# Output products of a Strassen scheme in fp32, with the weights standing or moving, and a transpose before the store

## The chip, the cores and the metric

The kernel runs on one core of a Trainium2 chip. The time is the device time of one execution in microseconds (us), and the kernel before takes 1200.21 us, the median of 3 runs (1199.89 to 1200.61).

The core's engines each take their own instructions in order and wait for one another by semaphores. TensorE (PE) multiplies: it loads an operand of 128x128 that stands (PEld, the weight load), and another one, up to 512 columns here, moves through it. Results go to PSUM banks of 128x512 values. VectorE (DVE) and ScalarE (ACT) take them on from there, GpSimd (POOL) and SyncE (SP) mostly issue DMAs.

## The reference

Batches of tokens go through an attention with a small state, then through two feed-forward parts (B = 8, 512 tokens and 32 state rows a batch, 512 features, inner sizes 2048 and 1024):

```python
x = attention(x, state)                    # (8 * 544, 512)
h = np.maximum(x @ w_in, 0.0)
x = h * h @ w_out                          # 4352 x 512
a = x @ w1
b = x @ w2
out = (a * b @ w3) @ w_out2                # 4352 x 512, float32
```

## The kernel before

Everything is float32. A product is made from HI and LO parts: HI is the value cast to the short form fp32r (a cast on ScalarE, L83), LO is the remainder (a subtraction on VectorE, L84). Three passes, HI·HI, LO·HI and HI·LO, make up a product (`PASSES`). Both halves of that are written into one tile; this is called a split.

The kernel has four stages: attention, the first feed-forward part (L586), the merging of w3 and w_out2 into one matrix w34 (L1123), and the last part, which takes the final 380 us or so. Only that last part is touched.

In it, batches go in pairs (c0, c1), four of them: (3,4), (5,6), (7,2), (0,1). The inner dimension of 1024 is taken in two halves, s = 0 and s = 1; the second goes through the pairs backwards, so that its pairs 1 to 4 are (0,1), (7,2), (5,6), (3,4). Each pair does two things:

- Four **quads** (`quad`, m = 0 to 3), which make a·b for 128 of the 512 inner features of the half and the tokens of a pair. A quad is a Strassen scheme of seven products, each six matmuls with 512 columns (L1301), into the banks A (qa), D (qd), E (qe) and C (qc). ScalarE copies a sum out (L1309, tiles s0 to s3), VectorE adds another bank to it (L1313), multiplies two of them into q1 and q0 (L1333, L1341), and forms differences of them (L1255).
- **out_pair**, the product of a·b with w34, again Strassen with seven products over pairs of batches and halves of the 256 output columns (NH): A11·B11, S1·T1, S4·B22, A12·B21, S2·T2, S3·T3, A22·T4, in that order, into banks oa, od, oe and oc. Each has 24 matmuls with 256 columns (L1461): the tokens' operand z stands and the weights move. Its operands z (B11, T1, B22, B21, and later T2, T3, T4) exist for idx 0, from the quads m = 0 and 1, and for idx 1, from m = 2 and 3. Their splits are made by `to_z` and `late_z` in six tiles c1 to c6, each holding one operand at a time.

Results of 128 tokens x 256 columns, two to a tile of 128x512, are collected in PSUM, copied out (L1484), added to (L1491) and stored. In the first half the pair that comes first goes to a scratch and is added in by the last pair of the second half, which loads it (`fetch`). All other pairs go to the output in the first half (L1499, on SP) and in the second are accumulated into it by DMA (L1501, on POOL). For batches 0 and 1 (c < BLK) the tokens stand in another order in the tile than for the others.

During an out_pair, the loads and splits for the next pair's quads (`make_pair`, tiles yq) run as `jobs`. Some weights change place within an out_pair: `load_turn` overwrites part 1 of w34 (L1426) after S4·B22, for S3·T3.

The order of instructions on each engine is set by a scheduler while the kernel is built, within the waits that code gives (`tc.issue_after`) and those that tiles give when they are reused.

Of the kernel before, what the change touches and what calls it, by code (L numbers as in the profile page):

```python
# [8 lines left out]
F32 = mybir.dt.float32  # L9
# [4 lines left out]
ALU = mybir.AluOpType  # L14
# [6 lines left out]
def kernel(  # L21
# [17 lines left out]
    nc = tc.nc  # L39
    B, H, S, D = x.shape  # L40
# [5 lines left out]
    P = 128  # L46
# [1250 lines left out]
    def quad(c0, c1, m, behind=None):  # L1297
        def product(ps, w, v, first=True, last=True):
            for kt in range(2):
                for k, (wi, vi) in enumerate(PASSES):  # L1300
                    nc.tensor.matmul(  # L1301
                        ps, W[w, kt][:, wi, m * P:(m + 1) * P], Y[v, kt][:, vi, :],
                        start=(first and kt == 0 and k == 0), stop=(last and kt == 1 and k == 2),
                        skip_group_check=True,
                    )

        def kept(i, ps):
            t = bp.tile([P, 512], F32, tag=f"s{i}", bufs=1 + (i == 0), name=f"s{i}")
            left["copy"] = nc.scalar.copy(t, ps)  # L1309
            return t  # L1310

        def plus(t, ps):
            nc.vector.tensor_tensor(out=t, in0=ps, in1=t, op=ALU.add)  # L1313

        A, D, E, C = bank_m("qa"), bank_y(m % 2, "qd"), bank_y(2, "qe"), bank_y(3, "qc")
        product(A, "A11", "B11", last=False)
        p1 = kept(0, A)
        with tc.issue_after(behind.ins) if behind else nullcontext():
            product(D, "S1", "T1", last=False)
        p5 = kept(1, D)  # L1320
        with tc.issue_after(behind.ins) if behind else nullcontext():
            product(E, "A12", "B21")
        plus(p1, E)
        product(A, "S2", "T2", first=False, last=False)
        u2 = kept(2, A)
        product(D, "S4", "B22", first=False)
        plus(u2, D)
        product(C, "A22", "T4")
        product(A, "S3", "T3", first=False)
        u3 = kept(3, A)  # L1330
        plus(p5, A)
        q1 = bp.tile([P, 512], F32, tag="qd" if m % 2 else "qb", bufs=1 if m % 2 else 2, name="q1")
        nc.vector.tensor_tensor(out=q1, in0=u2, in1=p5, op=ALU.mult)  # L1333
        if parts and m in (0, 2):
            add_behind(q1[:, :1])
        plus(u3, C)
        if m % 2:
            q0 = bp.tile([P, 512], F32, tag="qc", bufs=2, name="q0")
        else:
            q0 = pa.tile([P, 512], F32, tag="r", bufs=2, name="q0")  # L1340
        nc.vector.tensor_tensor(out=q0, in0=p1, in1=u3, op=ALU.mult)  # L1341
        return to_z(m, q0, q1)
# [84 lines left out]

    OUTS = {"11": (0, 0), "12": (1, 0), "21": (0, 1), "22": (1, 1)}
    AT = {"11": ("s0", "s1"), "22": ("yo", "yo"), "12": ("r", "r"), "21": ("qc", "qc")}
    TWO = ("s0", "yo", "r", "qb", "qc")  # L1430

    def place(tag, name):
# [2 lines left out]

    def out_pair(c0, c1, s, jobs, last, first, more):
        ends = s == 1 and not more
        jobs, gate = list(jobs), left["copy"]

        def do(n):  # L1440
# [12 lines left out]
            return w34_t[u][:, {"A11": 0, "A12": 2, "A22": 3}.get(w, 1)]  # L1453

        def product(ps, w, v, first=True, last=True):
            for tp in range(2):
                for t in (2 * tp, 2 * tp + 1):
                    for idx in range(NB):
                        rhs = moving(w, s * NB + idx, idx)
                        for k, (vi, wi) in enumerate(PASSES):  # L1460
                            nc.tensor.matmul(  # L1461
                                ps[tp][:, t % 2 * NH:(t % 2 + 1) * NH], Z[v, idx][:, vi, t * P:(t + 1) * P], rhs[:, wi],
                                start=(first and t % 2 == 0 and idx == 0 and k == 0), stop=(last and idx == NB - 1 and k == 2),
                                skip_group_check=True,
                            )
# [10 lines left out]
        def keep(block, ps, tp0=0):  # L1476
            ts = []
            for tp, p in enumerate(ps, tp0):
                if ends:
                    t = o_in.pop((block, tp))  # L1480
                    nc.vector.tensor_tensor(out=t, in0=p, in1=t, op=ALU.add)
                else:
                    t = place(AT[block][tp], "o")
                    nc.scalar.copy(t, p)  # L1484
                ts.append(t)
            return ts

        def put(block, ts, ps, tp0=0):
            c, i = where(block)
            for tp, t in enumerate(ts, tp0):  # L1490
                nc.vector.tensor_tensor(out=t, in0=ps[tp - tp0], in1=t, op=ALU.add)  # L1491
                if s == 0 and first:
                    nc.sync.dma_start(scr(c, i, tp), t)
                    continue
                rows_t = "(p j) e -> p j e" if c < BLK else "(j p) e -> p j e"
                dst = out[c * T:c * T + S, i * NH:(i + 1) * NH].rearrange(rows_t, j=J)[:, 2 * tp:2 * tp + 2]
                src = t.rearrange("p (j e) -> p j e", j=2)
                if s == 0 or ends:
                    nc.sync.dma_start(dst, src)  # L1499
                else:  # L1500
                    nc.gpsimd.dma_start(dst, src, accum_op=ALU.add)  # L1501

        for block in ("11", "22"):
            fetch(block)
# [155 lines left out]
```

## Time and profile before

| | |
|---|---|
| median of 3 runs | 1200.21 us (1199.89 to 1200.61) |
| the profiled execution | 1200.36 us, of which the span is 1198.5 us |
| granted TensorE clock over the span | 0.999 |
| TensorE busy | 1187.9 us |
| VectorE busy | 934.0 us |
| ScalarE busy | 694.4 us |

The page of the profile first gives the busy time of each engine, then the chain of waits that ended last, as a share of the span. Timelines show when each group of instructions begins, how long it lasts from its first start to its last end, and what the idle time before it waited for. PE's matmuls overlap, so that the distance from start to start is what counts there. Weight loads have rows of their own, PEld.

### The profile page before, as it was taken

What the parts mean: (1) busy time and instruction counts of PE and PEld (TensorE: products, weight loads), DVE (VectorE), ACT (ScalarE), POOL (GpSimd) and SP (SyncE); (2) the same over time, 40 slices, a digit from 0 to 9 for tenths busy, and PEclk for the clock granted to TensorE, in tenths of its full rate; (3) what the DMA queues carried; (4) which work ended last, traced back from release to release, by engine and by line L of the source; (5) the groups of instructions that cost most, each with busy time, mean ns of one, the idle gap of its engine ahead of it and who ended that gap; (6) DMA issues with size and microseconds to landing.
All of it is one profiled execution on the core that took longest, in us unless ns stands there. A gap on an engine that the chain in (4) does not pass through costs nothing.

```text
span 1198.5 us, 18846 instructions
## 1 busy us (share of the span) xinstructions
PE 1187.9 (99%) x6988; PEld 981.0 (82%) x6988; DVE 934.0 (78%) x1671; ACT 694.4 (58%) x1263; POOL 160.9 (13%) x225
## 2 busy tenths in 40 slices
PE   7999999999999999999999999999999999999998
PEld 5677777777777777777888888989898989898988
DVE  7989878778878673677778986969696958787877
ACT  6877556555556565777767653636454525354542
POOL 0000013324331100013221001010000001211210
PEclk9999999999999999999999999999999999999999
DMA  8675768946795923356697686574141631625334
GB/s 252 137 231 195 186 216 226 198 126 179 162 219 155 265 100 110 107 120 110 97 210 231 239 217 119 138 125 133 47 152 34 214 112 38 139 45 131 58 66 142
DMA packets 172533, 179.25 MB, mean 150 GB/s; under 512 B 90760, under 2 KB 124296, under 8 KB 171912
## 3 DMA queue, kind: packets, MB, share of 16 engines
q1 hardware_dynamic: 132936, 112.75, 32.0%
q0 software_dynamic: 37488, 61.88, 24.8%
q10 hardware_dynamic: 2016, 3.41, 0.8%
q8 instruction: 55, 0.90, 0.3%
q14 instruction: 38, 0.31, 0.1%
HBM read 114.43 MB, written 74.06 MB: 157 GB/s over the span
## 4 chain that ended last, share of the span: by engine, by line
PE 97%; ACT 1%; DVE 1%; DMA 0%; issue 0%; SPq 0%; DVEq 0%
PE y L586 22%; PE qa L1301 11%; PE qd L1301 7%; PE oa L1461 6%; PE od L1461 4%; PE ps_w L1123 4%; PE qc L1301 4%; PE qe L1301 4%; PE qa L957 3%; PE ps_sw L499 3%; PE oe L1461 2%; PE ab L1367 2%; PE qd L957 2%; PE oc L1461 2%; PE y L558 1%; PE po L1400 1%
## 5 line engine op out<-in xcount | busy, mean ns | idle before, releaser
L586 PE MATMUL y<-ghl,wo 128*128 128x512 f32 x1152 | 280.1, 392 | 0.1
L586 PEld LDWEIGHTS y<-ghl,wo 128*128 128x128 f32 x1152 | 214.3, 188 | 58.0 <-issue 12.6
L1309 ACT COPY s<-qa 128x512 f32<-128x512 f32 x96 | 56.4, 588 | 179.4 <-PE qa L1301 179.4
L1301 PE MATMUL qa<-yq,wq 128*128 128x512 f32 x576 | 143.9, 389 | 0.0
L530 DVE TENSOR_TENSOR ghl<-r,ghl 128x512 fp32r<-128x512 f32 (+1 forms) x112 | 72.6, 648 | 72.9 <-ACT ghl L529 63.7
L1301 PEld LDWEIGHTS qa<-yq,wq 128*128 128x128 f32 x576 | 107.6, 188 | 21.9
L1301 PE MATMUL qd<-yq,wq 128*128 128x512 f32 x384 | 97.4, 389 | 0.0
L84 DVE TENSOR_TENSOR z<-q,z 128x512 fp32r<-128x512 f32 x112 | 74.2, 686 | 24.3 <-ACT z L83 24.3
L1301 PEld LDWEIGHTS qd<-yq,wq 128*128 128x128 f32 x384 | 72.1, 188 | 15.0
L83 ACT CAST z<-q 128x512 fp32r<-128x512 f32 x112 | 68.2, 626 | 19.7 <-PE oe L1461 7.4
L1313 DVE TENSOR_TENSOR s<-qa,s 128x512 f32<-128x512 f32 x32 | 22.1, 692 | 69.8 <-ACT s L1309 69.8
L1501 POOL DMA_DIRECT2D out_dram<-o x24 | 28.8, 1617 | 310.3 <-DVE o L1491 310.3
L528 ACT ACTIVATE r<-r 128x512 f32<-128x512 f32 (+1 forms) x112 | 67.5, 603 | 4.2 <-DVE yo L597 1.5
L529 ACT CAST ghl<-r 128x512 fp32r<-128x512 f32 (+1 forms) x112 | 66.1, 591 | 2.8
L84 DVE TENSOR_TENSOR yq<-yraw,yq 128x512 fp32r<-128x512 f32 x98 | 64.2, 684 | 1.1 <-ACT yq L83 1.1
L83 ACT CAST yq<-yraw 128x512 fp32r<-128x512 f32 x98 | 59.2, 625 | 7.9 <-DVE yraw L1230 5.5
L1301 PE MATMUL qe<-yq,wq 128*128 128x512 f32 x192 | 48.7, 389 | 0.0
L1301 PE MATMUL qc<-yq,wq 128*128 128x512 f32 x192 | 48.7, 389 | 0.0
L1123 PE MATMUL ps_w<-wo,w3T 128*128 128x512 f32 x192 | 44.1, 390 | 0.0
L1255 DVE TENSOR_TENSOR q<-q,q 128x512 f32<-128x512 f32 x64 | 43.1, 684 | 0.0
L1301 PEld LDWEIGHTS qe<-yq,wq 128*128 128x128 f32 x192 | 36.0, 188 | 7.5
L1301 PEld LDWEIGHTS qc<-yq,wq 128*128 128x128 f32 x192 | 36.0, 188 | 7.5
(708 smaller groups left out, 2503.4 us busy)
## 6 DMA issues: line engine op xcount, KB each, us to landing
yraw<-yscr SPq DMA_DIRECT2D x56, 256.0 KB, 5.6
raw<-in_moe_w_out_dram SPq DMA_DIRECT2D x16, 512.0 KB, 4.6
yscr<-yo SPq DMA_DIRECT2D x32, 256.0 KB, 3.3
raw<-in_moe_w_dram POOLq DMA_DIRECT2D x64, 128.0 KB, 4.0
raw<-in_moe_w_dram POOLq DMA_DIRECT2D x16, 512.0 KB, 7.7
raw<-in_moe_w_in_dram SPq DMA_DIRECT2D x12, 512.0 KB, 4.4
xb<-in_x_dram SPq DMA_DIRECT2D x96, 64.0 KB, 3.1
X<-in_x_dram SPq DMA_DIRECT2D x12, 512.0 KB, 9.0
```

What stands on the lines that cost most here:

```text
L83: nc.scalar.copy(hi, src)
L84: return nc.vector.tensor_tensor(out=lo, in0=src, in1=f32(hi), op=ALU.subtract)
L528: nc.scalar.activation(r[:, :n], r[:, :n], ACTF.Square)
L529: casts.append(nc.scalar.copy(t[:, HI, :n], r[:, :n]))
L530: done.append(nc.vector.tensor_tensor(out=t[:, LO, :n], in0=r[:, :n], in1=f32(t[:, HI, :n]), op=ALU.subtract))
L586: mm = nc.tensor.matmul(y_ps[c, d][:, :n], wo_t[f][:, wi, d * P:(d + 1) * P], t[:, gi, :n], start=(f == f0 and k == 0), stop=(f == f1 - 1 ...
L957: nc.tensor.matmul(ps[d], wt[:, wi, d * P:(d + 1) * P], v[:, kt, gi, :], start=(first and kt == 0 and k == 0), stop=(last and kt == 1 and ...
L1123: mm = nc.tensor.matmul(ps, t[:, wi, (j % 4) * P:(j % 4 + 1) * P], wo2_t[j][:, vi, :], start=(j == 0 and k == 0), stop=(j == N1 - 1 and k ...
L1255: return nc.vector.tensor_tensor(out=t, in0=a, in1=b, op=ALU.subtract)
L1301: nc.tensor.matmul(ps, W[w, kt][:, wi, m * P:(m + 1) * P], Y[v, kt][:, vi, :], start=(first and kt == 0 and k == 0), stop=(last and kt == ...
L1309: left["copy"] = nc.scalar.copy(t, ps)
L1461: nc.tensor.matmul(ps[tp][:, t % 2 * NH:(t % 2 + 1) * NH], Z[v, idx][:, vi, t * P:(t + 1) * P], rhs[:, wi], start=(first and t % 2 == 0 an ...
```

## The change

For three of the four pairs of each half (in the code `turn`: all but the first of the first half, and the last of the second, which go on as before) the product's operands change roles. The weights stand: 128 of 256 columns of w34, every second one, in two groups d = 0, 1. The tokens' z moves, 512 columns at once. So a product has 12 matmuls with 512 columns instead of 24 with 256, and results lie with the columns on partitions and the tokens along the tile.

The first half's turned results go to the scratch, and the second half accumulates the scratch into its own tile (POOL, L1523). A tile is then turned, in the quads m = 0 (blocks 11 and 12) and m = 1 (22 and 21) of the pair that follows: `turn_out` transposes it in 32x32 blocks on VectorE (L1440) into a tile "turned", whose tags are c6, c5, c4 and c2, and stores it in four DMAs on SP (L1443), each with runs of 64 values (256 bytes). In all 24 transposes of 128x512 and 48 such stores.

```diff
@@ -1329,6 +1329,8 @@
         product(A, "S3", "T3", first=False)
         u3 = kept(3, A)
         plus(p5, A)
+        for block in to_turn[:2]:
+            turn_out()
         q1 = bp.tile([P, 512], F32, tag="qd" if m % 2 else "qb", bufs=1 if m % 2 else 2, name="q1")
         nc.vector.tensor_tensor(out=q1, in0=u2, in1=p5, op=ALU.mult)
         if parts and m in (0, 2):
@@ -1427,6 +1429,18 @@
 
     OUTS = {"11": (0, 0), "12": (1, 0), "21": (0, 1), "22": (1, 1)}
     AT = {"11": ("s0", "s1"), "22": ("yo", "yo"), "12": ("r", "r"), "21": ("qc", "qc")}
+    TURNED = {"11": 6, "12": 5, "22": 4, "21": 2}
+    to_turn = []
+
+    def turn_out():
+        block, c, i, ts = to_turn.pop(0)
+        o = bp.tile([P, 4 * J, NS, 2], F32, tag=f"c{TURNED[block]}", bufs=1, name="turned")
+        for d, t in enumerate(ts):
+            src = t.rearrange("p (j k n) -> p k n j", j=J, n=NS // J) if c < BLK else t
+            nc.vector.transpose(out=o[:, :, :, d], in_=src)
+        dst = out[c * T:c * T + S, i * NH:(i + 1) * NH].rearrange("(k p) (a e) -> a p k e", p=NS, a=4)
+        for a in range(4):
+            nc.sync.dma_start(dst[a], o[a * NS:(a + 1) * NS].rearrange("p k e d -> p k (e d)"))
     TWO = ("s0", "yo", "r", "qb", "qc")
 
     def place(tag, name):
@@ -1435,6 +1449,7 @@
 
     def out_pair(c0, c1, s, jobs, last, first, more):
         ends = s == 1 and not more
+        turn = not ends and not (s == 0 and first)
         jobs, gate = list(jobs), left["copy"]
 
         def do(n):
@@ -1453,6 +1468,17 @@
             return w34_t[u][:, {"A11": 0, "A12": 2, "A22": 3}.get(w, 1)]
 
         def product(ps, w, v, first=True, last=True):
+            if turn:
+                for d in range(2):
+                    for idx in range(NB):
+                        lhs = moving(w, s * NB + idx, idx).rearrange("p i (n d) -> p i d n", d=2)
+                        for k, (vi, wi) in enumerate(PASSES):
+                            nc.tensor.matmul(
+                                ps[d], lhs[:, wi, d], Z[v, idx][:, vi, :],
+                                start=(first and idx == 0 and k == 0), stop=(last and idx == NB - 1 and k == 2),
+                                skip_group_check=True,
+                            )
+                return
             for tp in range(2):
                 for t in (2 * tp, 2 * tp + 1):
                     for idx in range(NB):
@@ -1480,7 +1506,8 @@
                     t = o_in.pop((block, tp))
                     nc.vector.tensor_tensor(out=t, in0=p, in1=t, op=ALU.add)
                 else:
-                    t = place(AT[block][tp], "o")
+                    tag = "tp" if turn and s == 1 and AT[block][tp] == "s1" else AT[block][tp]
+                    t = place(tag, "o")
                     nc.scalar.copy(t, p)
                 ts.append(t)
             return ts
@@ -1489,16 +1516,18 @@
             c, i = where(block)
             for tp, t in enumerate(ts, tp0):
                 nc.vector.tensor_tensor(out=t, in0=ps[tp - tp0], in1=t, op=ALU.add)
-                if s == 0 and first:
+                if s == 0 and (first or turn):
                     nc.sync.dma_start(scr(c, i, tp), t)
+                    continue
+                if turn:
+                    nc.gpsimd.dma_start(t, scr(c, i, tp), accum_op=ALU.add)
                     continue
                 rows_t = "(p j) e -> p j e" if c < BLK else "(j p) e -> p j e"
                 dst = out[c * T:c * T + S, i * NH:(i + 1) * NH].rearrange(rows_t, j=J)[:, 2 * tp:2 * tp + 2]
                 src = t.rearrange("p (j e) -> p j e", j=2)
-                if s == 0 or ends:
-                    nc.sync.dma_start(dst, src)
-                else:
-                    nc.gpsimd.dma_start(dst, src, accum_op=ALU.add)
+                nc.sync.dma_start(dst, src)
+            if turn and s == 1:
+                to_turn.append((block, c, i, ts))
 
         for block in ("11", "22"):
             fetch(block)
```

The order of the engines changes in these places. On ScalarE, at the start of the output products of the second pair of the second half, in before (q is a quad's product, z its split; z_10742 and z_10746 are B11 and T1 for idx 1):

```order
L1309 COPY s0_10759<-qa_10749 128x512
L1309 COPY s1_10767<-qd_10750 128x512
L83 CAST z_10742<-q0_10740 128x512
L1309 COPY s2_10782<-qa_10749 128x512
L83 CAST z_10746<-q0_10740 128x512
L1309 COPY s3_10803<-qa_10749 128x512
L83 CAST yq_10880<-yraw_10599 128x512
L83 CAST yq_10883<-yraw_10600 128x512
L1484 COPY o_10839<-oa_10813 128x512
L83 CAST yq_10932<-yraw_10599 128x512
```

and in after (z_10387 is B22 for idx 0, z_10636 is T4 for idx 0, z_10458 is B11 for idx 1):

```order
L1309 COPY s3_10519<-qa_10465 128x512
L83 CAST yq_10572<-yraw_10301 128x512
L83 CAST yq_10575<-yraw_10302 128x512
L83 CAST yq_10612<-yraw_10301 128x512
L83 CAST z_10387<-q1_10382 128x512
L83 CAST yq_10615<-yraw_10302 128x512
L83 CAST z_10586<-q0_10292 128x512
L83 CAST yq_10670<-yraw_10301 128x512
L83 CAST z_10547<-q1_10522 128x512
L83 CAST z_10636<-q0_10385 128x512
L83 CAST yq_10673<-yraw_10302 128x512
L83 CAST z_10458<-q0_10456 128x512
```

The casts for B11 and T1 for idx 1, which stood between the copies of the last quad, now stand eleven and twelve rows behind its last copy s3 (T1's is the row after the last one shown).

On TensorE, at the same place, in before (oa and od are the banks of A11·B11 and S1·T1; z_10592 is B11 for idx 0, z_10742 for idx 1):

```order
L1301 MATMUL qa_10749<-yq_10524,wq_9774 128x512 x3
L1301 MATMUL qa_10749<-yq_10527,wq_9777 128x512 x3
L1461 MATMUL oa_10813<-w34b_9780,z_10592 128x256 x3
L1461 MATMUL oa_10813<-w34b_9782,z_10742 128x256 x3
...
L1461 MATMUL oa_10814<-w34b_9780,z_10592 128x256 x3
L1461 MATMUL oa_10814<-w34b_9782,z_10742 128x256 x3
```

and in after:

```order
L1476 MATMUL oa_10529<-z_10294,w34b_9552 128x512 x3
L1476 MATMUL oa_10530<-z_10294,w34b_9552 128x512 x3
L1476 MATMUL od_10554<-z_10298,s12_9724 128x512 x3
L1476 MATMUL od_10555<-z_10298,s12_9724 128x512 x3
L1476 MATMUL oe_10618<-z_10392,w34b_9552 128x512 x3
L1476 MATMUL oe_10619<-z_10392,w34b_9552 128x512 x3
L1476 MATMUL oc_10698<-z_10636,w34b_9552 128x512
L1476 MATMUL oc_10699<-z_10636,w34b_9552 128x512
L1476 MATMUL oa_10529<-z_10458,w34b_9554 128x512 x3
L1476 MATMUL oa_10530<-z_10458,w34b_9554 128x512 x3
L1476 MATMUL od_10554<-z_10462,s12_9727 128x512 x3
L1476 MATMUL od_10555<-z_10462,s12_9727 128x512 x3
```

idx 0 and idx 1 no longer alternate. What needs idx 0 of B11 (z_10294), T1 (z_10298) and B21 (z_10392) stands ahead, two matmuls of A22·T4 follow, and then idx 1 of A11·B11 and S1·T1 (z_10458, z_10462).

On VectorE, in the first quad of the same pair, in before:

```order
L1313 TENSOR_TENSOR s2_10563<-qd_10531,s2_10563 128x512
L1313 TENSOR_TENSOR s1_10548<-qa_10530,s1_10548 128x512
L1313 TENSOR_TENSOR s3_10584<-qc_10533,s3_10584 128x512
L1333 TENSOR_TENSOR q1_10587<-s2_10563,s1_10548 128x512
L1341 TENSOR_TENSOR q0_10590<-s0_10540,s3_10584 128x512
L84 TENSOR_TENSOR z_10592<-q0_10590,z_10592 128x512
```

and in after (o_10029 and o_10031 are the tiles of block 11, o_10148 and o_10150 those of 12):

```order
L1313 TENSOR_TENSOR s2_10251<-qd_10219,s2_10251 128x512
L1440 STREAM_TRANSPOSE turned_10275<-o_10029 128x512
L1313 TENSOR_TENSOR s1_10236<-qa_10218,s1_10236 128x512
L1440 STREAM_TRANSPOSE turned_10275<-o_10031 128x512
L1440 STREAM_TRANSPOSE turned_10282<-o_10148 128x512
L1440 STREAM_TRANSPOSE turned_10282<-o_10150 128x512
L1335 TENSOR_TENSOR q1_10289<-s2_10251,s1_10236 128x512
L1313 TENSOR_TENSOR s3_10272<-qc_10221,s3_10272 128x512
L1313 TENSOR_TENSOR s0_10321<-qe_10313,s0_10321 128x512
L1343 TENSOR_TENSOR q0_10292<-s0_10228,s3_10272 128x512
```

Four transposes now stand between the quad's additions and its products q1 and q0.

## Rows read from the trace of the kernel before

**Rows 1.** The page: span, busy time and share of each engine, chain
```profile
span 1198.5 us, 18846 instructions
...
PE 1187.9 (99%) x6988; PEld 981.0 (82%) x6988; DVE 934.0 (78%) x1671; ACT 694.4 (58%) x1263; POOL 160.9 (13%) x225
...
PE 97%; ACT 1%; DVE 1%; DMA 0%; issue 0%; SPq 0%; DVEq 0%
```

**Rows 2.** Windows: length, busy us of PE, PEld, DVE, ACT, POOL, clock, DMA share, GB/s
```profile
1057.25:1077.40 20.15, 20.15 (x169) 20.15 (x168) 19.34 (x33) 14.51 (x27) 3.85 (x4) 1.00 0.31 55
1019.10:1057.25 38.15, 38.15 (x171) 31.59 (x169) 27.19 (x45) 14.38 (x25) 5.75 (x5) 1.00 0.48 107
```

**Rows 3.** Timeline of PE: start, length, engine, line, operation
```profile
1055.89 1.52 PE L1301 MATMUL qa<-yq,wq 128*128 128x512 f32 x6
1057.25 3.04 PE L1461 MATMUL oa<-w34b,z 128*128 128x256 f32 x24
1060.12 3.04 PE L1461 MATMUL od<-s,z 128*128 128x256 f32 x24
```

**Rows 4.** Timeline of ACT, last quads and first output products
```profile
1051.13 0.62 ACT L83 CAST z<-q 128x512 fp32r<-128x512 f32 x1
...
1053.85 0.62 ACT L83 CAST z<-q 128x512 fp32r<-128x512 f32 x1
...
1057.45 0.59 ACT L1309 COPY s<-qa 128x512 f32<-128x512 f32 x1 [2.98 <-PE qa L1301]
1057.93 1.14 ACT L83 CAST yq<-yraw 128x512 fp32r<-128x512 f32 x2
1058.97 0.59 ACT L1484 COPY o<-oa 128x512 f32<-128x512 f32 x1
```

**Rows 5.** Timeline of DVE, first output products
```profile
1058.07 0.69 DVE L1313 TENSOR_TENSOR s<-qa,s 128x512 f32<-128x512 f32 x1 [2.27 <-ACT s L1309]
1058.67 0.68 DVE L1313 TENSOR_TENSOR s<-qc,s 128x512 f32<-128x512 f32 x1
1059.27 0.68 DVE L1333 TENSOR_TENSOR q<-s,s 128x512 f32<-128x512 f32 x1
```

**Rows 6.** Weight loads in one pair, by line: busy us, mean ns | idle
```profile
L1301 PEld LDWEIGHTS qd<-yq,wq 128*128 128x128 f32 x48 | 9.0, 188 | 1.9
...
L1461 PEld LDWEIGHTS od<-s,z 128*128 128x128 f32 x24 | 3.0, 192 | 0.0
```

**Rows 7.** Line 296, transposes in the attention stage: ns min/median/max
```profile
L296 DVE STREAM_TRANSPOSE xT<-xb x24: 666/700/712, 63.7 to 410.6; 128x512 f32<-128x512 f32 x24
```

**Rows 8.** Timelines of POOL, DVE, ACT and PE in a pair's first quads
```profile
1020.65 4.82 POOL L1501 DMA_DIRECT2D out_dram<-o  x4 [0.62 <-DVE o L1491]
...
1030.71 0.68 DVE L1333 TENSOR_TENSOR q<-s,s 128x512 f32<-128x512 f32 x1
...
1031.61 0.59 ACT L1309 COPY s<-qd 128x512 f32<-128x512 f32 x1 [0.77 <-PE qd L1301]
...
1034.13 1.52 PE L1301 MATMUL qd<-yq,wq 128*128 128x512 f32 x6
```

**Rows 9.** Line 1501, the accumulating DMAs
```profile
DMA to landing us min/median/max: 4.3/6.6/9.5
```

**Rows 10.** Line 301, loads of X of 512 KB
```profile
DMA to landing us min/median/max: 4.8/9.0/15.0
```

**Rows 11.** DMA from 8 to 20 us, loads of X and a weight
```profile
DMA packets 6225, 3.19 MB, mean 266 GB/s; under 512 B 5446, under 2 KB 5446, under 8 KB 6224
```

**Rows 12.** DMA from 1042 to 1057 us
```profile
DMA packets 0, 0.00 MB, mean 0 GB/s; under 512 B 0, under 2 KB 0, under 8 KB 0
```

**Rows 13.** Line 1426, reloads of the weights that turn
```profile
DMA to landing us min/median/max: 3.1/3.9/7.6
```

**Rows 14.** Timeline of all engines, start of the last pair's output products
```profile
1173.77 3.04 PE L1461 MATMUL oa<-w34b,z 128*128 128x256 f32 x24
...
1174.59 0.69 DVE L1313 TENSOR_TENSOR s<-qa,s 128x512 f32<-128x512 f32 x1 [2.27 <-ACT s L1309]
```

## The prediction

> **What bounds the kernel now.** First the page's busy shares and its chain of waits: TensorE is busy 99% of a span of 1198.5 us and carries 97% of the chain, and no other engine has more than 78% [rows 1]. So a saving on TensorE counts in full, and so does each wait that it is given. Then the windows of one pair: 20.15 us of output products, all of it TensorE, with VectorE busy 19.34 of them; and four quads in 38.15 us, with VectorE at 27.19 [rows 2]. VectorE thus has 11 us of room in the quads and under one in the output products. Last the timelines around the start of such a phase, where the order of ScalarE and VectorE decides when TensorE gets its next operand [rows 3 to 5]. I follow the second pair of the second half, whose output products begin at 1057.25.
>
> **Fewer and longer matmuls.** A product of 24 matmuls with 256 columns goes from 1057.25 to 1060.12, 2.87 us or 120 ns each; six with 512 columns go from 1055.89 to 1057.25, 227 ns each [rows 3]. Twelve of those take 2.72 us. I take 0.16 us a product (the whole phase gives the same: 20.15 against 84 x 0.227 = 19.04 us), and six turned pairs of seven products make 42: **-6.7 us**.
> The Trainium skill ("TensorE: Matmul & The Clock Gate", Back-to-back issue gap) gives an isolated warm spacing of N/2.4 + 2.5 ns, 109 and 216 ns here; an estimate from it is 2.62 against 2.59 us a product, 1.2 us in all, and the sum below would be +10.0. It adds that a stream with weight loads goes otherwise; the rows, with 120 and 227, decide for this kernel.
>
> **Weights with a stride.** The standing operand is now every second column, 8 bytes apart; no load of before is like it. Today's loads take 188 to 192 ns and already follow at 120 ns in the output products [rows 3, 6]. Lower bound: nothing. Upper bound: twice the time, a pitch of 240 instead of 227 ns, 13 ns x 504 = +6.6 us. A gain is excluded, since a load of the same 128 columns isn't the limit at 227. I take nothing, because a load at 120 ns has 107 ns to spare under a 512-column matmul.
>
> **Transposes.** 24 of them, four blocks for each of three pairs, two tiles a block. The kernel has the same operation on the same shape, in its attention stage, at 0.70 us [rows 7]: 16.8 us of VectorE, 5.6 in each of three groups of quads, which go from 27.2 to 32.8 busy of 38.15. The order puts them in quads 0 and 1. In quad 0 the product q1, at 1030.71 in before [rows 8], comes three transposes later, near 1032.5 at its end; ScalarE's next copy into s1 (1031.61 before) must wait for it and ends near 1033.2, and TensorE adds to that bank at 1034.13 [rows 8]. About 0.9 us of slack is left, so 0; if the cover were gone, the cost would be some tenths in each of the three pairs.
>
> **Stores and accumulation.** The first half stores its three turned pairs to scratch instead of the output, same bytes on the same queue: 0. In the second half POOL's accumulation now goes into the tile. It takes 4.3 to 9.5 us to land today [rows 9]; a pair's last four are issued from 1020.65 to 1025.5 [rows 8], at most 9.5 us later they are in, and quad 1, which turns their blocks, ends near 1038 (38.15 / 4 a quad): 0. The 48 new stores of 128 KB have 256-byte runs, and the tile each leaves (c6, c5, c4, c2) is overwritten by a split of the same pair. Near them are the loads of X, also 256-byte runs: 512 KB land in 9.0 us at the median [rows 10], and a window full of such packets, 5446 of 6225, moved 3.19 MB in 12 us [rows 11]. A pair's 2.1 MB would need 8 us at that rate; they are issued from about 1031 on, and the DMA queues are empty from 1042 to 1057 [rows 12]. I take them as done by 1054, before the splits that follow: 0. Nothing below 0 is to be had from any of this, since none of it stands on TensorE's path now.
>
> **Splits that move.** This is the term that decides. Because the turned tiles lie in c2, c4 and c5, the scheduler puts the splits of B11 and T1 for idx 1, and of B22 for idx 0, behind the last quad wherever the quads carry transposes: pairs 2, 3 and 4 of the second half. In before ScalarE casts two of them at 1051.13 and 1053.85, long ahead of the first output product [rows 4]. In after they stand behind the copy s3 and a run of ten casts. The engines take their work in order, so that is the price:
> - ScalarE begins s3 at 1057.45, the next cast at 1057.93, and two casts take 1.04 us up to 1058.97, so 0.52 each [rows 4].
> - TensorE fills with 18 matmuls on operands that are there: 18 x 0.227 = 4.08, to 1061.33. Then come two that need the ninth cast (T4), which starts at 1057.93 + 8 x 0.52 = 1062.09 and ends 0.62 later: **1.4 us of waiting**. They last till 1063.16.
> - B11 needs the eleventh cast, started at 1063.13 and done at 1063.75: **0.6**. Its LO part is VectorE's, done 0.69 later, after one matmul of 0.23: **0.5**. Five more matmuls last till 1065.6.
> - T1's LO part stands four VectorE operations behind B11's. At their pitch of 0.60 (1058.07, 1058.67, 1059.27) [rows 5] it starts at 63.75 + 2.4 = 1066.15 and ends at 1066.85; TensorE has one HI matmul to do and is there at 1065.8: **1.1**.
> - The weights that turn are reloaded after S4·B22 and needed by S3·T3, 18 matmuls or 4.1 us later instead of 5.7; the reload lands in 3.1 to 7.6, median 3.9 [rows 13]: 0 to 3.5, I take **0.3**, near the median.
> Sum 3.9 us. The next pair has the same list, but one cast ahead (T2, into the tile that holds T1 of idx 0) waits for TensorE to have read that, near 1060: +0.5, **4.4**. In the last pair the columns stay 256: its 18 matmuls of fill last only 2.2 us, to 1173.77 + 2.16 = 1175.9, and two more to 1176.2; B11's LO half is the sixth on VectorE from 1174.59 [rows 14], so 1174.59 + 3.0 + 0.69 = 1178.3: 2.1, and 0.8 more where B21's LO comes late: **2.9**. Together **+11.2 us**. From half of it (fill that I count too short, casts in another order) to one and a half: 5.6 to 16.8.
> In the first half and in pair 1 of the second nothing is postponed, and the order there is as before: 0.
>
> **Sum.** -6.7 + 11.2 = +4.5. The profiled execution took 1200.36 us (span 1198.5 and 1.86 around it) and the median is 1200.21, 0.15 less; from the profile 1204.9, from the median **1204.7 us**. Some 0.2%, 2.4 us, is what a measurement of this kernel can tell from no change.
>
> **The rivals.**
> - *No stall (faster).* The splits are covered: ScalarE gets through its ten casts before the fill ends. Only the -6.7 stands: **1193.5 us**. For it: ScalarE is busy 14.51 of 20.15 us in this phase [rows 2], so it has the time, and a trace may show that casts ahead of z were ready long before and ran in the gaps of the last quad. Against it: the order is fixed, s3 waits for the last quad's bank until 1057.45, and eleven casts would have to take 0.35 us each to be in time where the rows show 0.52. It decides below 0.35. Chance 0.11.
> - *Half of the stall.* The waits overlap with one another or with the next quads: 5 to 9 us of stall, 1198.5 to 1202.6. It is the same mechanism at a smaller price, chance 0.14.
> - *Strided weights at twice the time.* +6.6 on top: **1211.3 us**. For it: nothing in the trace is like it. Against: loads hide at 120 ns now. It decides once a load sets a pitch above 227 ns. Chance 0.08.
> - *Short-run stores late.* If the 512 KB blocks go one after another at X's 9.0 us [rows 10], the fourth is stored at 1031 + 4 x 9 = 1067, and the cast into c2 starts then and not at 1063.1: +3.7, the same in the next pair, +6.4 in the last, whose fill is shorter: **1218.5 us**. For it: X's landings reach 15.0 us [rows 10]. Against: several were in flight there at once, and the queues are empty for 15 us here. Chance 0.05. The Trainium skill ("DMA: Bandwidth & Descriptors", Specifications) asks for at least 512 bytes for line rate and has a read-modify-write below it, which would make writes slower than these reads; no row here shows a store in such runs.
>
> **How the numbers follow.** Forecast 0.62 (1202.6 to 1210), half 0.14, no stall 0.11, strided 0.08, stores 0.05. Faster by over 0.2%: no stall and the lower end of half, 0.13. Within it: the rest of half and the forecast's lowest edge, 0.15. Slower: 0.72. The range 1198 to 1212 leaves out no stall, late stores and the far ends, under 0.2.
>
> **What would show it.** In the trace of after: twelve matmuls a product at 227 ns in the first half, phases near 19.0 us; loads near 190 ns. In the second half, from pair 2 on, TensorE idle some 4 us in the first half of the output products, released by ScalarE's and VectorE's split (z). Transposes at 0.70 us inside the quads with no wait of TensorE on them. The forecast is wrong if those phases show no idle TensorE (then 1193.5), if the casts into c2 and c4 wait for a DMA (then 1218), or if the pitch is over 235 ns (then 1211).

## The result, and the profile after

The changed kernel takes 1211.18 us, the median of 5 runs (1210.14 to 1212.79), against 1200.61 (1199.89 to 1200.77) of the kernel before: 1.009 times, 95% interval 1.0075 to 1.0105. It is slower by 10.6 us where the prediction had 4.5. The profiled execution took 1211.18 us too, its span is 1209.3.

The page of the changed kernel, its busy shares and its chain of waits:

```profile
PE 1190.0 (98%) x6484; PEld 957.7 (79%) x6484; DVE 952.9 (79%) x1695; ACT 695.5 (58%) x1263; POOL 152.9 (13%) x225
...
PE 93%; DVE 3%; ACT 2%; DMA 1%; issue 1%; SPq 0%; ACTq 0%; DVEq 0%
```

Beside [rows 1], TensorE's share of the chain has fallen from 97% to 93%, and VectorE and ScalarE have moved in. Windows of four phases of output products, pairs 1, 2, 3 and 4 of the second half (columns as in [rows 2]):

```profile
997.53:1017.13 19.60, 19.60 (x86) 16.20 (x84) 18.39 (x31) 14.51 (x27) 2.62 (x3) 1.00 0.24 50
1056.63:1080.28 23.65, 21.18 (x87) 16.08 (x85) 20.39 (x33) 16.44 (x30) 1.93 (x3) 1.00 0.16 39
1118.30:1142.76 24.46, 21.19 (x87) 16.08 (x85) 20.39 (x33) 16.54 (x30) 1.94 (x3) 1.00 0.16 41
1180.80:1205.10 24.30, 22.14 (x169) 21.70 (x167) 21.66 (x36) 6.90 (x12) 0.00 (x0) 0.93 0.49 158
```

Pair 1, where nothing is postponed, takes 19.60 us with TensorE busy throughout; before, such a phase took 20.15 [rows 2]. Pairs 2 and 3 take 23.65 and 24.46, one quad matmul of 0.23 among each, so 3.8 and 4.6 over pair 1. Pair 4, whose products are as before, takes 24.3 where the kernel before needs 20.4, from 1173.77 [rows 14] to the end of its last matmuls (timeline of PE, before):

```profile
1192.23 1.96 PE L1554 MATMUL oc<-w34b,z 128*128 128x256 f32 x15
```

The timeline of PE in pair 2 shows where the 3.8 us lie (start, length, operation, and in brackets the idle time ahead and what ended it):

```profile
1056.63 1.56 PE L1476 MATMUL oa<-z,w34b 128*128 128x512 f32 x6
1058.03 1.56 PE L1476 MATMUL od<-z,s 128*128 128x512 f32 x6
1059.43 1.56 PE L1476 MATMUL oe<-z,w34b 128*128 128x512 f32 x6
1062.17 0.74 PE L1476 MATMUL oc<-z,w34b 128*128 128x512 f32 x2 [1.18 <-ACT z L83]
1063.21 0.51 PE L1476 MATMUL oa<-z,w34b 128*128 128x512 f32 x1 [0.30 <-ACT z L83]
1063.94 1.43 PE L1476 MATMUL oa<-z,w34b 128*128 128x512 f32 x5 [0.22 <-DVE z L84]
1065.31 0.50 PE L1476 MATMUL od<-z,s 128*128 128x512 f32 x1
1066.59 1.43 PE L1476 MATMUL od<-z,s 128*128 128x512 f32 x5 [0.78 <-DVE z L84]
```

It is the list of the prediction: 18 matmuls on idx 0, a wait for T4's cast, one for B11's cast, one for its LO half, one for T1's. Read by starts the waits are longer than the bracketed idle: 18 matmuls at 0.233 end their share at 1060.83, and the next starts at 1062.17, 1.34 us later. The others, read in the same way, are 0.57, 0.50 and 1.05, with 0.2 more ahead of T1's first matmul.

One wait was not in the sum. TensorE is in quad 1 of pair 2, and VectorE still has two transposed blocks ahead of quad 0's q1 (timelines of DVE, ACT and PE):

```profile
1028.99 3.09 DVE L1440 STREAM_TRANSPOSE turned<-o 128x512 f32<-128x512 f32 x3
1032.00 0.65 DVE L1335 TENSOR_TENSOR q<-s,s 128x512 f32<-128x512 f32 x1
...
1032.74 0.58 ACT L1309 COPY s<-qd 128x512 f32<-128x512 f32 x1 [3.89 <-DVE q L1335]
...
1033.38 1.65 PE L1301 MATMUL qd<-yq,wq 128*128 128x512 f32 x6 [1.12 <-ACT s L1309]
```

These transposes take 1.10 us each, against 0.70 in [rows 7]; in a row they follow one another at about 1.0 us (ns, minimum, median and maximum of the eight in these quads):

```profile
L1440 DVE STREAM_TRANSPOSE turned<-o x8: 1065/1102/1123, 1027.1 to 1040.4; 128x512 f32<-128x512 f32 x8
```

The quads of pair 2 last 39.5 us (1017.13 to 1056.63) instead of 38.1.

Put together, measured against predicted:

| term | predicted | measured |
|---|---|---|
| six turned phases, without waits | -6.7 | 6 x (19.60 - 20.15) = -3.3 |
| quads of pair 2 | 0 | +1.4 |
| waits in the output products of pair 2 | +3.9 | +3.8 |
| of pair 3 | +4.4 | +4.6 |
| of pair 4 | +2.9 | +3.9 |
| sum | +4.5 | +10.4 |

The spans differ by 10.8 us; the last 0.4 lie in small shifts elsewhere.

### The profile page after: what moved, and what is told of

It reads as the page before. It is cut to its first block, busy times and chain, and to the rows that moved or that the text cites. A ratio compares the mean times of both kernels' runs of the same rounds, so it can differ in the third digit from the quotient of the medians.

```text
span 1209.3 us, 17962 instructions
## 1 busy us (share of the span) xinstructions
PE 1190.0 (98%) x6484; PEld 957.7 (79%) x6484; DVE 952.9 (79%) x1695; ACT 695.5 (58%) x1263; POOL 152.9 (13%) x225
## 4 chain that ended last, share of the span: by engine, by line
PE 93%; DVE 3%; ACT 2%; DMA 1%; issue 1%; SPq 0%; ACTq 0%; DVEq 0%
PE y L586 20%; PE qa L1301 11%; PE qd L1301 7%; PE oa L1476 4%; PE ps_w L1123 4%; PE qc L1301 4%; PE qe L1301 3%; PE qa L957 3%; PE od L1476 3%; PE ps_sw L499 3%; PE ab L1369 2%; PE qd L957 2%; PE oa L1487 1%; PE oc L1476 1%; PE y L558 1%; PE oe L1476 1%
## 5 line engine op out<-in xcount | busy, mean ns | idle before, releaser
L1301 PEld LDWEIGHTS qd<-yq,wq 128*128 128x128 f32 x384 | 71.8, 188 | 16.8 <-ACT s L1309 1.9
L1523 POOL DMA_DIRECT2D o<-oscr x24 | 20.8, 1056 | 325.9 <-DVE o L1518 322.8
```

The lines of the kernel that those rows point to most:

```text
L1301: nc.tensor.matmul(ps, W[w, kt][:, wi, m * P:(m + 1) * P], Y[v, kt][:, vi, :], start=(first and kt == 0 and k == 0), stop=(last and kt == ...
```

## The experiments

The theory: the order of the engines costs the waits, because the turned tiles lie in c2, c4 and c5 and the scheduler thinks that their stores hold these long; the stores, the transposes and the weights themselves don't. Rivals: the stores really hold the tiles, or the transposes or the strided weights cause the waits. Two smaller questions are why a matmul takes 233 instead of 227 ns and why some transposes take 1.10 us.

**Without the stores.**

```diff
         for a in range(4):
-            nc.sync.dma_start(dst[a], o[a * NS:(a + 1) * NS].rearrange("p k e d -> p k (e d)"))
+            pass
```

> The changed kernel without its 48 new stores of turned tiles (those rows of the output are not written); the transposes stay. With the stores gone the scheduler leaves the splits of B11, T1 and B22 in their old place between the copies of the last quad. Theory (order): the waits of 3.8, 4.6 and 3.9 us in the output products of pairs 2, 3 and 4 of the second half vanish, 12.3 us, and the time goes from 1211.2 to about 1199; the 1.3 us in quad 1 of pair 2 stays. Rival (the transposes or the strided weights cause the waits): within 2 us of the changed kernel.

Measured: 1199.27 us, 0.9987 of the kernel before (0.9978 to 0.9997). The splits stand between the copies again, and pairs 2 and 3 take the 19.6 us of pair 1, without a wait (windows of those two phases):

```profile
1056.29:1075.88 19.59, 19.59 (x86) 16.20 (x85) 18.40 (x31) 14.51 (x27) 2.58 (x3) 1.00 0.25 51
1114.18:1133.78 19.60, 19.60 (x86) 16.21 (x85) 18.40 (x31) 14.51 (x27) 2.58 (x3) 1.00 0.24 51
```

So the 24 transposes and the strided weights, both still there, don't make the waits in the output products; the wait of 1.12 us in quad 1 of pair 2 stayed. Whether the stores make them by traffic or by the order is left to the next one.

**The order held, the stores in place.** The scheduler is told (`issue_after`) to queue some instructions behind others of their engine. The last line holds each output matmul behind the one before it.

```diff
-            left["copy"] = nc.scalar.copy(t, ps)
+            with behind_split({(3, 2): ("B11", 1), (3, 3): ("T1", 1)}.get((m, i))):
+                left["copy"] = nc.scalar.copy(t, ps)
...
-        nc.vector.tensor_tensor(out=q1, in0=u2, in1=p5, op=ALU.mult)
+        with behind_split({3: ("T1", 1, LO)}.get(m)):
+            nc.vector.tensor_tensor(out=q1, in0=u2, in1=p5, op=ALU.mult)
...
+                            with behind_mm():
```

> The changed kernel with all its stores where they are; only the order is held: casts of B11 and T1 for idx 1 ahead of the copies s2 and s3 of the last quad, their LO halves ahead of q1 on VectorE, and the output matmuls in the order written. Theory (the order alone costs it; the tiles are free, since the stores land in about 3 us): as without the stores, 1211.2 - 12.3, about 1199. Rival (the stores hold c2, c4 and c5): the casts then wait for a DMA in the last quad and the time stays over 1206.

Measured: 1201.09 us, 1.0002 of before (0.9993 to 1.0012), 10 us less than the changed kernel with every store in place. In pair 2 the cast of T1 waits for its operand on VectorE, not for a DMA, and in the changed kernel itself the DMA queues are all but empty after the stores (timeline of ACT here, then two rows of the changed kernel: its DMA line from 1046 to 1057, and the landing of the 48 stores):

```profile
1056.07 0.62 ACT L83 CAST z<-q 128x512 fp32r<-128x512 f32 x1 [2.17 <-DVE q L1269]
```

```profile
DMA packets 19, 0.00 MB, mean 0 GB/s; under 512 B 19, under 2 KB 19, under 8 KB 19
...
DMA to landing us min/median/max: 2.3/3.0/4.9
```

In the changed kernel the stores land in 2.3 to 4.9 us and are over soon after 1046, some twelve microseconds before the first of the casts that were put off (1058.87). So the cost is the order alone: it comes with the stores, goes when they are left out, and goes when it is held with the stores in place. That the scheduler reckons with stores that hold the tiles long is the likely reason for its order, and not shown. Nor do the runs show which of the three engines' orders costs how much, since all were held together. What is left over the 1199 expected is one wait in the last pair, which my own order caused there by holding S4·B22 ahead of A12·B21 (timeline of PE):

```profile
1181.73 4.63 PE L1508 MATMUL od<-w34b,z 128*128 128x256 f32 x24 [2.13 <-DVE opart L1528]
```

These 24 matmuls took 4.44 us from start to start (the next begin at 1186.17) instead of 2.88: after the wait the granted clock was 0.50, 1.2 GHz, from 1183 to 1186. This profile is of an execution of 1203.03 us, 1.9 over the median.

**Adjacent columns.** The standing weights are 128 adjacent columns.

```diff
-                        lhs = moving(w, s * NB + idx, idx).rearrange("p i (n d) -> p i d n", d=2)
+                        lhs = moving(w, s * NB + idx, idx).rearrange("p i (d n) -> p i d n", d=2)
```

> The changed kernel with standing weights of 128 adjacent columns instead of every second one, which writes the features of an output row in another order; the order of instructions is the same. Theory (the stride sets the pitch of 233 ns): the pitch falls to the 227 of the quads, 504 x 6.5 ns = 3.3 us, to about 1208, and weight loads fall from 193 to 188 ns. Rival (something else in these products, such as what moves or where it is read): pitch stays 233 ns and the time within 1 us of 1211.2.

Measured: 1208.47 us, 2.7 less than the changed kernel in other runs (1.0068 of before, 1.0049 to 1.0086). This interval overlaps that of the changed kernel (1.0075 to 1.0105), so the time alone doesn't show the gain; the trace does. The pitch falls from 233 to 227 ns and the loads from 193 to 188 ns (PE timeline of pair 2 of the first half: products start 2.73 and 2.71 apart; then weight loads: busy us, mean ns, idle, of this phase and of the changed kernel from 780 to 980):

```profile
807.39 2.88 PE L1476 MATMUL oa<-z,w 128*128 128x512 f32 x12
810.12 2.88 PE L1476 MATMUL od<-z,s 128*128 128x512 f32 x12
812.83 2.99 PE L1476 MATMUL od<-z,w 128*128 128x512 f32 x12
```

```profile
L1476 PEld LDWEIGHTS oa<-z,w 128*128 128x128 f32 x24 | 4.5, 188 | 0.9
...
L1476 PEld LDWEIGHTS oa<-z,w 128*128 128x128 f32 x72 | 13.9, 193 | 2.9
```

So the stride sets the pitch, and it costs 12 x 6.5 ns a product. By what path it does so stays open.

**Transposes read straight along the tile.** The tiles of batches 0 and 1 have their tokens in another order, and the transpose reads them rearranged; here it doesn't.

```diff
-            src = t.rearrange("p (j k n) -> p k n j", j=J, n=NS // J) if c < BLK else t
+            src = t
```

> The changed kernel with the transposes of batches 0 and 1 read straight along the tile like those of the other batches, which writes their tokens in another order; the order of instructions is the same. Theory (the rearranged source makes these eight transposes 1.03 us instead of 0.70, and so the wait of 1.1 us of TensorE for ScalarE's copy s1 in quad 1 of pair 2): transposes all at 0.70 us, no wait there, 1.3 us less, about 1210. Rival (four transposes in a quad are too many at any length): the wait stays above 0.8 us.

Measured: 1209.46 us, 1.7 less (1.0078 of before, 1.0061 to 1.0095; again too little to be told by the time alone). All 24 transposes take 0.70 us (ns, minimum, median and maximum; the maximum was 1123), and of the wait in quad 1 about 0.1 us is left:

```profile
L1440 DVE STREAM_TRANSPOSE turned<-o x24: 670/703/711, 1026.3 to 1161.9; 128x512 f32<-128x512 f32 x24
```

The quads of pair 2 last 38.3 us (1016.39 to 1054.69), 1.2 less than in the changed kernel.

**The order held better.** As the second experiment, in the last pair for the first two products alone, and with the transposes asked for after q0.

```diff
-        for block in to_turn[:2]:
-            turn_out()
         q1 = bp.tile([P, 512], F32, tag="qd" if m % 2 else "qb", bufs=1 if m % 2 else 2, name="q1")
...
+        for block in to_turn[:2]:
+            turn_out()
         return to_z(m, q0, q1)
```

> The changed kernel with the order held as in e2_splits_first, but in the last pair for A11·B11 and S1·T1 alone, and with the transposes asked for after a quad's q1 and q0, so that only one of four stands ahead of q1. Theory: against e2_splits_first (1201.1) the wait of 2.1 us for VectorE in the last pair and that of 1.1 to 1.3 us in quad 1 of pair 2 go: about 1197.7, faster than before by 0.25%. Rival (the transposes only push the wait elsewhere on VectorE, whose room in the quads they need): 1199.5 or more, with TensorE waiting for z or s in the quads.

Measured: 1199.54 us, 0.9993 of before (0.9984 to 1.0002), 1.8 above my number. It is the rival's number, and as the rival had it TensorE waits for s in a quad. The big waits are gone; small ones have come in their place (timeline of PE, all idle time of the second half after its first quad):

```profile
1043.35 1.66 PE L1315 MATMUL qd<-yq,wq 128*128 128x512 f32 x6 [0.63 <-ACT s L1324]
...
1180.40 0.38 PE L1508 MATMUL oa<-s,z 128*128 128x256 f32 x1 [0.20 <-DVE opart L1528]
1181.00 0.98 PE L1508 MATMUL oe<-w34b,z 128*128 128x256 f32 x6 [0.22 <-DVE z L84]
```

They make up about 1 us; the rest of the 1.8 stays open. The change, done without its big waits, makes no difference that can be told from none.

**Columns sorted too.** w34 is stored with its even columns first, so that the standing weights are adjacent and the output keeps its order. Where w34 moves (the pairs not turned, and the state rows), it is read interleaved, one column of each half in turn (`back`). The helpers `cols_2` and `evens` view a tile as two halves, and as its even and odd columns.

```diff
+    def back(t):
+        return t.rearrange("p (d n) -> p n d", d=2)
...
-        split(t[:, :, HI], t[:, :, LO], v)
+        split(cols_2(t[:, :, HI]), cols_2(t[:, :, LO]), evens(v))
...
-                        lhs = moving(w, s * NB + idx, idx).rearrange("p i (n d) -> p i d n", d=2)
+                        lhs = moving(w, s * NB + idx, idx).rearrange("p i (d n) -> p i d n", d=2)
...
-                                ps[tp][:, t % 2 * NH:(t % 2 + 1) * NH], Z[v, idx][:, vi, t * P:(t + 1) * P], rhs[:, wi],
+                                    ps[tp][:, t % 2 * NH:(t % 2 + 1) * NH], Z[v, idx][:, vi, t * P:(t + 1) * P], back(rhs[:, wi]),
```

> As e5_order_held, and w34 is stored with its even columns first and then its odd ones, so that the standing weights are adjacent columns and the output keeps its order; the products that were not turned, and those of the state rows, read the moving weights with the two halves interleaved. Theory (pitch): 3.3 us less than e5_order_held, about 1194.4, if moving weights with a stride cost nothing. Rival: interleaved moving weights slow these 2 x 168 and 2 x 24 matmuls from 120 ns and 227 ns; at one and a half times the time they cost 336 x 60 + 48 x 113 ns = 26 us, and the time is about 1220.

Measured: 1195.71 us, 0.9958 of before (0.9945 to 0.9972). This beats both kernels by a little. The interleaved read was no cost but a gain (timeline of PE, the first pair of the first half, which isn't turned): two products start 2.67 us apart, 111 ns a matmul, where it was 2.87 and 120 [rows 3].

```profile
749.21 2.84 PE L1524 MATMUL oa<-w,z 128*128 128x256 f32 x24
751.88 2.84 PE L1524 MATMUL od<-s,z 128*128 128x256 f32 x24
```

This gain in two pairs (14 products of 0.2 us, 2.8) and the adjacent columns (3.3) should have given 6.1 us over the run before it; 3.8 came, and the rest stays open.

**The kernel before, with w34 read interleaved.** Nothing is turned; w34 is stored as in the last experiment.

```diff
-        split(t[:, :, HI], t[:, :, LO], v)
+        split(cols_2(t[:, :, HI]), cols_2(t[:, :, LO]), evens(v))
...
-                                ps[tp][:, t % 2 * NH:(t % 2 + 1) * NH], Z[v, idx][:, vi, t * P:(t + 1) * P], rhs[:, wi],
+                                ps[tp][:, t % 2 * NH:(t % 2 + 1) * NH], Z[v, idx][:, vi, t * P:(t + 1) * P], back(rhs[:, wi]),
```

> The kernel before, with nothing turned; only w34 stored with even columns first and read back with the two halves interleaved as the operand that moves, as in e6_order_and_columns, where such products took 2.67 instead of 2.88 us. Theory (the interleaved read itself makes the pitch 111 instead of 120 ns): eight pairs x 7 products x 0.2 us = 11 us less at most, 1189; VectorE, busy 19.34 of 20.15 us there, may hold back up to half of it, 1195. Rival (it was the first half's other order, not the read): products stay at 2.87 us and the time within 1 us of 1200.4.

Measured: 1196.96 us, 0.9968 (0.9957 to 0.998). Its products take 2.67 us, so it is the read; of the 11 us in them 3.8 arrive, less than I allowed. TensorE now waits for VectorE at bank E of the next quads, which it didn't in the kernel before (timeline of PE, then its waits from 700 to 1195: engine and line, for what, us in total, times, longest):

```profile
1054.57 2.84 PE L1477 MATMUL oa<-w34b,z 128*128 128x256 f32 x24
1057.24 2.84 PE L1477 MATMUL od<-s,z 128*128 128x256 f32 x24
...
PE qe L1316 <- DVE o L1507: 2.2, 6, 0.4
```

So in this form, too, the turned products of the last experiment (1195.71) are worth about a microsecond, which these runs hardly tell apart.

**The quads' tokens interleaved as well,** in the kernel before and in the turned one.

```diff
-                split(t[:, HI], t[:, LO], src(kt))
+                split(cols_1(t[:, HI]), cols_1(t[:, LO]), evens1(src(kt)))
...
-                        ps, W[w, kt][:, wi, m * P:(m + 1) * P], Y[v, kt][:, vi, :],
+                        ps, W[w, kt][:, wi, m * P:(m + 1) * P], back(Y[v, kt][:, vi, :]),
```

> As e7_before_interleaved, and the quads' moving tokens are stored and read in the same interleaved way. Theory: the quads' matmuls fall from 227 to 218 ns too, 1344 x 9 ns = 12 us less than e7_before_interleaved, if the split of the tokens, which now reads with a stride, keeps its 0.62 and 0.68 us. Rival (a matmul of 512 columns gains nothing): pitch 227 ns in the quads and the time of e7_before_interleaved.

> e6_order_and_columns with the quads' moving tokens interleaved. Theory: 12 us less than e6_order_and_columns (1195.7), 1184, unless VectorE, which also has the transposes there, becomes late: then between. Rival: 1195.7.

Measured: 1195.76 us not turned (0.9957, 0.9942 to 0.9972) and **1188.78 us** turned (0.9894, 0.9878 to 0.9911), the fastest kernel here. Of the 12 us expected of each, 1.2 came where nothing is turned and 6.9 in the turned kernel. The quads' matmuls fall to 216 ns in both (six in 1.29 to 1.30 us; timeline of PE, not turned):

```profile
741.27 1.46 PE L1316 MATMUL qe<-yq,wq 128*128 128x512 f32 x6
742.57 1.46 PE L1316 MATMUL qa<-yq,wq 128*128 128x512 f32 x6
```

The condition of the expectation didn't hold: the split of the tokens, which now reads with a stride, takes 0.80 and 0.79 us at the mean where the kernel before has 0.62 and 0.68 (nothing turned: busy us, mean ns, idle; in the turned kernel 0.74 and 0.76):

```profile
L83 ACT CAST yq<-yraw 128x512 fp32r<-128x512 f32 x98 | 74.7, 803 | 18.1 <-DVE yraw L1245 15.0 <-DMA yraw<-yscr 3.1
L84 DVE TENSOR_TENSOR yq<-yraw,yq 128x512 fp32r<-128x512 f32 x98 | 74.8, 794 | 2.2 <-ACT yq L83 2.2
```

What the quads bring is mostly eaten by waits where nothing is turned: VectorE is late with the sums from bank E, and TensorE waits for that bank in six pairs, and for ScalarE's copies too (waits from 700 to 1195 as above, not turned), but for bank E only once in the turned kernel (the second two):

```profile
PE qe L1316 <- DVE o L1507: 7.6, 6, 1.3
PE od L1477 <- ACT o L1500: 3.0, 6, 0.5
```

```profile
PE qd L1330 <- ACT s L1339: 1.7, 2, 1.4
PE qe L1330 <- DVE o L1555: 1.3, 1, 1.3
```

In the turned kernel's other pairs the order has a second A product whole ahead of the E product, 1.3 us more cover. Whether that is all of the 7 us between the two, with the shorter splits there, was not tried.

## Why the prediction was right, and where it fell short

- **Splits that move: right.** The step of the two small lists was the case: 3.8 and 4.6 us measured for 3.9 and 4.4, and the four waits for splits where the sum has them. The fifth term, 0.3 for the weights that are reloaded, was not there; 0.2 ahead of T1's first matmul stood in its place. Holding the order alone took 10 us off. For the last pair the sum had 2.9 and 3.9 were measured. The wait for B11's LO half was 2.16 there as predicted (2.1), but after 2.5 us with hardly any matmul the granted clock of TensorE fell to half of full speed, 1.2 for 2.4 GHz (windows of the changed kernel; the clock is the third number from the end):

```profile
1183.06:1185.60 2.54, 0.40 (x4) 0.19 (x2) 2.47 (x5) 0.00 (x0) 0.00 (x0) 1.00 0.02 6
1186.30:1187.30 1.00, 1.00 (x7) 1.00 (x6) 0.98 (x2) 0.62 (x1) 0.00 (x0) 0.50 0.86 315
1187.30:1188.30 1.00, 1.00 (x7) 1.00 (x6) 1.00 (x3) 0.00 (x0) 0.00 (x0) 0.50 1.01 369
1189.50:1190.50 1.00, 1.00 (x11) 1.00 (x10) 1.00 (x3) 0.35 (x1) 0.00 (x0) 1.00 0.00 0
```

  16 matmuls then took 3.32 us (1185.62 to 1188.94) instead of 16 x 0.12 = 1.92, 1.4 us that no term had. The clock fell in the last pair of three of the four profiles with such a wait (this one, the one with the order held first, and the one with plain transposes). In the fourth, with adjacent columns, the same wait of 2.16 us stood there and the granted clock was 1.00 throughout (1182 to 1190); there TensorE then did wait for B21's LO half, the 0.8 of the sum, which in the changed kernel the slow matmuls covered. That profile has its half clock in pairs 2 and 3 instead (timeline of PE, then windows, with adjacent columns):

```profile
1189.11 0.73 PE L1487 MATMUL oe<-w34b,z 128*128 128x256 f32 x4 [0.58 <-DVE z L84]
...
1182.00:1190.00 8.00, 5.42 (x41) 5.13 (x42) 7.90 (x14) 2.90 (x5) 0.00 (x0) 1.00 0.31 100
1064.00:1066.00 2.00, 1.57 (x5) 0.93 (x4) 2.00 (x5) 1.14 (x3) 0.00 (x0) 0.50 0.01 4
```

- **Fewer and longer matmuls: half the size.** The term -6.7 came from 227 ns, the pitch of loads of adjacent columns. I gave the strided weights nothing within bounds of 0 and +6.6; they cost 3.3 us, in the middle. The argument that a load of 188 ns that follows at 120 hides under a matmul of 227 was the failing step: loads got 5 ns longer (193) and the pitch 6, though by the 107 ns to spare neither should have shown. Adjacent columns gave the 227 ns back. The rival of strided weights at twice the time gave 1211.3, which is the time measured, but by luck: its sign, a pitch over 235 ns, wasn't there, and half of its 6.6 us was.
- **Transposes: the 0 failed for one pair.** The 0.70 us was read from a transpose that reads along the tile; eight of the 24 read rearranged tiles and took 1.10. The wait came on the path that the prediction followed, q1 of quad 0, ScalarE's copy into s1, TensorE's next bank. The slack of 0.9 us there was enough for 0.70: without the rearrangement the wait all but vanished. It cost 1.4 us.
- **Stores: right.** They landed in 2.3 to 4.9 us, quicker than X's loads had me fear. The rival of late stores had no case here. Nor had the rule about runs under 512 bytes that the prediction has from the Trainium skill ("DMA: Bandwidth & Descriptors", Specifications): whatever it costs a store, no engine waited for one.
- **No stall, and half of it:** the first one's condition, casts of at most 0.35 us, didn't hold, and the waits didn't overlap as the second had it: 12.3 us, not 5 to 9. The price of no stall was near: 1199.3 without the stores, less the 3.3 and 1.4 us of the two misses above, is 1194.6 for its 1193.5.

So the waits came for the reason given and nearly at the size given, but the total is 10.6 us for 4.5. The time lies at the upper end of the range (1198 to 1212), above the band that I thought likeliest (1202.6 to 1210), since the three misses, 3.4, 1.4 and 1.0 us, went the same way. That it still lies inside is partly luck: the room on that side was mostly for longer waits of the same kind (up to 16.8 us), and other things filled it.

## What to carry to other kernels

When tiles are reused, ask where a scheduler puts the work that waits for them, and not only when the tile is really free: here splits were put 11 us later beside stores that had long landed, and the order alone cost 10 us. An operand's access pattern has a price of its own, and it can go either way: strided standing weights and rearranged transposes cost time here, an interleaved moving operand gained some. Take a duration only from a row with the same access pattern. And a wait of some microseconds on TensorE can cost more than its length, since the clock may fall after it, as it did in the last pair of three profiles and not in a fourth.

## What the runs showed of the hardware

Matmuls whose moving operand is read interleaved, one value from each of two halves 512 bytes (or 1 KB) apart, follow one another faster than with the same operand read along: 111 ns for 256 columns instead of 120, 216 ns for 512 instead of 227, at a granted clock of 1.00 (2.4 GHz). The Trainium skill ("TensorE: Matmul & The Clock Gate", Back-to-back issue gap) has an isolated spacing of N/2.4 + 2.5 ns, by estimate 109 and 216 here: the interleaved rows agree with it within 2%, the others, by which I dismissed it, don't. Why reading along is slower wasn't tried. A transpose of 128x512 takes 0.70 us read along the tile and 1.10 read rearranged. A load of 128 columns beside matmuls of 512 takes 193 ns with columns 8 bytes apart and 188 ns adjacent; beside matmuls of 256 it took 192 with adjacent columns [rows 6], so the stride is not all that sets it.
